# Attention products on 64-column tiles, one logarithm for two head pairs, and other norms

## The chip, the cores and the metric

The kernel runs on one core of one Trainium2 chip. A core has a matrix engine (TensorE, PE in the profile; its weight loads are shown as PEld), three engines for vectors (VectorE, DVE; ScalarE, ACT; GpSimd, POOL), a queue engine (SyncE, SP) and 16 DMA engines. The engines run side by side, each through its own instructions in the order in which they were written, and wait for one another by semaphores. Matmuls read SBUF and write PSUM, which has eight banks of 512 floats per partition. The metric is device time in microseconds (us). The median of three runs of the kernel before is 380.99 us (380.83 to 381.56).

## The reference

Sparse attention, then a feed-forward layer with a periodic activation. Eight batches, eight heads, 576 tokens, 64 columns a head; a token sees its neighbours within 32, and eight global tokens see and are seen by all.

```python
scores = scale * np.matmul(q, k.transpose(0, 1, 3, 2))
mask = np.abs(pos[:, None] - pos[None, :]) <= window
mask = mask | is_global[:, None] | is_global[None, :]
scores = np.where(mask, scores, -1000000000.0)
attn = np.exp(scores - max);  attn = attn / (sum(attn) + 1e-09)
x = np.matmul(attn, v)                  # heads side by side: 4608 x 512
h = x @ w_in                            # 512 x 2048
s = np.sin(alpha * h)
g = h + s * s / (alpha + 1e-09)
out = g @ w_out                         # 2048 x 512
```

## The kernel before, in words

The work goes batch by batch. `attention(b)` makes `xT`, the attention output of batch b with columns on the partitions and the 576 tokens along the free side, in four chunks of 128 columns (two heads, a "head pair", each). `gemm1(b)` multiplies it with `w_in` in 16 groups `nt` of 128 columns, and makes from each the activation in `H2`. `gemm2(b)` multiplies that with `w_out`; it is a generator that gives one matmul of 512 columns at each call, 64 for an even batch and 80 for an odd one. `fill(n)` takes n of them, so the second product of batch b-1 is strewn among the instructions of `attention(b)` and `gemm1(b)`. The counts are written out by hand (`START`, `PER_SCORES`, `LATE`, `MIDST`, `PER_GROUP`, `GROUP_LATE`). What is left over is run after the last batch. There is no planner: the order of the program text is the order on each engine.

Attention takes the keys in 12 blocks of 48, each with the eight global keys and for two heads at once (128 partitions), against 60 query positions of either parity, 120 columns. For head pair `hp` there are three groups `g` of four blocks. `scores(hp, g)` makes four matmuls into one of two `ring` banks (L739), ACT takes the exponential into `E` (L747) and adds it up along the free side into a column of `EA` (its accumulator is read by an instruction of its own), and DVE multiplies with a 0/1 mask (L750).

`products(hp, gs, keys)` (L781) multiplies `E` with the values `VX` (key 0, into PSUM tile `zn`) and with a block matrix of ones `OB` (key 1, the sums, into `zd`), 14 matmuls with 128 columns of weights per pair and key. The last pair uses `zd` and a third tile `zr` in the place of the ring. `inverse(hp)` takes Ln of the sums (L807) and Exp of its negative (L810), again with a row sum into `RA`; `normalise(hp)` (L813) multiplies on DVE into `xT`; `sums` (L791) gathers the parts of the global rows, whose quotient (L862, L863) is `XG`. The pair `hp - 1` is multiplied between the scores of pair `hp`, so one pair is always behind.

In `gemm1`, group `nt` uses `zn`, `zr`, `zd` in turn, the last group `zn`. PE writes a tile in eight matmuls (L969), ACT takes the sine (L1005), ACT or DVE squares it (L1010, L1012), and DVE adds both parts (L1016), which frees the tile. For the last batch 64 columns of global rows (`XG`, L974) ride along.

The sine is exact only for small arguments and the sums must be in range, so the kernel judges itself: `square_x` and `token_norms` (L899 to L910) make the squared norm of each token by squares on DVE and a matmul with ones, `square_w` and `column_norms` (L873, L880) that of each column of `w_in`; `judge` compares these and the row sums, and if they fail, a general path runs instead.

DMA: POOL's queue casts and loads k, q, v, `w_in` (`load_w_in`, L407) and `w_out`; SP's queue transposes k and q, spreads the global values and writes the output (L1042). DVE places the transposed k and q of the next batch (`place`, L347, L354); `beside(at)` puts that and the norms after pair `at`.

## Time and profile before

| | |
|---|---|
| median of three runs | 380.99 us |
| span of the profiled execution | 379.3 us |
| mean granted TensorE clock | 0.994 |
| PE busy | 338.6 us, 89% |
| ACT busy | 294.0 us, 77% |
| DVE busy | 288.8 us, 76% |
| POOL busy | 130.4 us, 34% |

The profiled execution is known by its span, from its first instruction to its last; what lies around it is not in the profile. A row of a group reads: line, engine, operation, output <- inputs, shapes, count | busy us, mean ns of one | idle us before it, and what ended it. A row of the timeline reads: start, duration, engine, line, operation, count, and in brackets the idle time before it with its releaser. Matmuls overlap, and the end of each is modelled, so the distance between starts tells what one costs when many follow each other. A row of busy time by stretch reads: start:end, length, then for PE, PEld, DVE, ACT and POOL busy us and (x instructions), the granted clock, the DMA share, and GB/s.

### The profile page before, as it was taken

The numbers are of one execution on the slowest core, as the hardware profiler recorded it, in microseconds if no ns is written. First come the engines' busy times: TensorE is split into PE (matmuls) and PEld (weight loads), VectorE is DVE, ScalarE is ACT, GpSimd is POOL, SyncE is SP. The second block draws the span as 40 slices with busy tenths as digits, with TensorE's granted clock in tenths as the row PEclk, the third lists the DMA queues.
The fourth block names the chain that finished last, engine by engine and source line by source line (L and its number), as shares of the span: only waits on it lengthen the run. The fifth ranks groups of instructions, "written<-read, shape, count | busy, mean of one in ns | idle before, by whom it ended". The sixth has DMA issues, their size and how long they took to land. (4 is left out here: it accounts for less than half of the span.)

```text
span 379.3 us, 8582 instructions
## 1 busy us (share of the span) xinstructions
PE 338.6 (89%) x3124; PEld 231.9 (61%) x3172; DVE 288.8 (76%) x615; ACT 294.0 (77%) x563; POOL 130.4 (34%) x203
## 2 busy tenths in 40 slices
PE   2578967998998899899989999999999998999893
PEld 2466645765566666676666766676676665775341
DVE  5787897589789887988888788888888876589400
ACT  6889797899889688788878887879788888675110
POOL 7981695677277002840086007720000000000001
PEclk9999999999999999999999999999999999999997
DMA  7998999999988772799069923828111010101221
GB/s 121 117 184 172 152 166 173 170 207 146 204 163 76 134 124 65 92 109 204 28 85 105 193 58 45 84 31 156 50 35 29 0 55 32 29 3 29 56 84 48
DMA packets 103579, 38.08 MB, mean 100 GB/s; under 512 B 94138, under 2 KB 98250, under 8 KB 103082
## 3 DMA queue, kind: packets, MB, share of 16 engines
q0 software_dynamic: 56640, 18.56, 42.2%
q1 hardware_dynamic: 46890, 18.89, 23.1%
q8 instruction: 27, 0.44, 0.5%
q14 instruction: 22, 0.18, 0.2%
HBM read 37.15 MB, written 17.83 MB: 145 GB/s over the span
## 5 line engine op out<-in xcount | busy, mean ns | idle before, releaser
L1029 PE MATMUL zo<-w_out,H 128*128 128x512 bf16 x528 | 142.5, 378 | 2.0
L969 PEld LDWEIGHTS <-w_in 128*128 128x128 bf16 x1024 | 99.2, 97 | 49.3 <-issue 17.6
L390 POOL DMA_DIRECT2D VX<-in_v_dram x128 | 84.0, 667 | 106.5 <-PE zd L781 89.6
L1029 PEld LDWEIGHTS <-H 128*128 128x128 bf16 x576 | 52.0, 97 | 37.3
L747 ACT ACTIVATE E<-ring 128x480 bf16<-128x480 f32 x96 | 54.2, 568 | 23.3 <-PE ring L739 22.8
L969 PE MATMUL zn<-xT,w_in 128*128 128x288 bf16 x384 | 57.3, 285 | 5.6 <-DVE H L1016 4.1
L969 PE MATMUL zr<-xT,w_in 128*128 128x288 bf16 x320 | 47.9, 285 | 1.3 <-DVE H L1016 0.6
L969 PE MATMUL zd<-xT,w_in 128*128 128x288 bf16 x320 | 46.6, 285 | 1.7 <-DVE H L1016 1.7
L750 DVE TENSOR_TENSOR E<-E,MASK 128x480 bf16<-128x480 bf16 x96 | 36.0, 408 | 14.8 <-ACT E L747 13.5
L1016 DVE SCALAR_TENSOR_TENSOR H<-s,recipT,zn 128x576 bf16<-128x576 bf16 x48 | 39.1, 814 | 10.5 <-ACT s L1010 6.2
L1005 ACT ACTIVATE sb<-zn,alphaT 128x576 bf16<-128x576 f32 (+1 forms) x48 | 35.6, 742 | 13.3 <-PE zn L969 9.8
L1057 POOL DMA_INDIRECT out_dram<-osb,grow x1 | 1.0, 1007 | 126.1 <-SPq L1158 126.1
L1010 ACT ACTIVATE s<-sb 128x576 bf16<-128x576 bf16 (+1 forms) x62 | 42.7, 689 | 2.0
L739 PE MATMUL ring<-QX,KX 128*128 128x120 bf16 x384 | 37.2, 221 | 7.1 <-ACT E L747 4.2
L739 PEld LDWEIGHTS <-KX 128*128 128x128 bf16 x384 | 28.2, 100 | 22.0 <-issue 9.0
L1016 DVE SCALAR_TENSOR_TENSOR H<-s,recipT,zd 128x576 bf16<-128x576 bf16 x40 | 32.5, 813 | 6.5 <-ACT s L1010 4.8
L1016 DVE SCALAR_TENSOR_TENSOR H<-s,recipT,zr 128x576 bf16<-128x576 bf16 x40 | 32.5, 813 | 5.0 <-ACT s L1010 2.8
L1012 DVE TENSOR_TENSOR s<-sb 128x576 bf16<-128x576 bf16 (+1 forms) x66 | 30.8, 467 | 7.0 <-ACT sb L1005 6.7
L1035 ACT COPY osb<-zo 128x512 f32<-128x512 f32 x36 | 20.8, 578 | 19.5 <-PE zo L1029 19.4
L1005 ACT ACTIVATE sb<-zd,alphaT 128x576 bf16<-128x576 f32 (+1 forms) x40 | 29.7, 742 | 7.5 <-PE zd L969 4.7
L1005 ACT ACTIVATE sb<-zr,alphaT 128x576 bf16<-128x576 f32 (+1 forms) x40 | 29.6, 740 | 5.1 <-PE zr L969 3.8
L781 PEld LDWEIGHTS <-VX 128*128 128x128 bf16 x448 | 25.9, 98 | 12.2 <-issue 6.7
(157 smaller groups left out, 446.8 us busy)
## 6 DMA issues: line engine op xcount, KB each, us to landing
VX<-in_v_dram POOLq DMA_DIRECT2D x128, 36.0 KB, 3.6
kd<-in_k_dram POOLq DMA_DIRECT2D x7, 576.0 KB, 6.2
qd<-in_q_dram POOLq DMA_DIRECT2D x7, 576.0 KB, 8.9
w_in<-in_moe_w_in_dram POOLq DMA_DIRECT2D x4, 512.0 KB, 5.7
w_out<-in_moe_w_out_dram POOLq DMA_DIRECT2D x4, 512.0 KB, 8.7
out_dram<-osb SPq DMA_DIRECT2D x8, 256.0 KB
out_dram<-osb SPq DMA_DIRECT2D x8, 224.0 KB
out_dram<-osb SPq DMA_DIRECT2D x8, 192.0 KB
```

The lines of the kernel that those rows point to most:

```text
L390: nc.gpsimd.dma_start(out=VX[b % 2][r : r + 24, hp, :, t * D : t * D + D], in_=v[b, 2 * hp + t].rearrange("(i a y) d -> y a i d", a=24, y= ...
L739: nc.tensor.matmul(out=ps[:, e * WCOL : (e + 1) * WCOL], lhsT=kx[:, hp, i, :], rhs=qx[:, hp, :, s0 : s0 + 60], start=True, stop=True, skip ...
L747: nc.scalar.activation(out=Eg, in_=ps[:, 0 : 4 * WCOL], func=AF.Exp, scale=scale, accum_out=EA[:, n : n + 1])
L750: nc.vector.tensor_tensor(out=Eg, in0=Eg, in1=MASK[:, 4 * g : 4 * g + 4, :].rearrange("p i c -> p (i c)"), op=ALU.mult,)
L781: nc.tensor.matmul(out=out_t[:, half, :, a - half * CUT : z - half * CUT], lhsT=OB[:] if key else VXb[:, hp, i, :], rhs=E[:, i, :, a - s0 ...
L969: nc.tensor.matmul(out=h[:, e, 0:HALF], lhsT=lhsT, rhs=xT[:, c, e, :], start=(c == 0), stop=(c == CT - 1), skip_group_check=True,)
L1005: nc.scalar.activation(out=sb[:, :, 0:W], in_=h[:, :, 0:W], func=AF.Sin, scale=alphaT[:, nt : nt + 1])
L1010: nc.scalar.activation(out=s2[:, :, 0:W], in_=sb[:, :, 0:W], func=AF.Square)
L1012: nc.vector.tensor_tensor(out=s2[:, :, 0:W], in0=sb[:, :, 0:W], in1=sb[:, :, 0:W], op=ALU.mult)
L1016: nc.vector.scalar_tensor_tensor(out=dst.rearrange("p (e c) -> p e c", e=2), in0=s2[:, :, lo:hi], scalar=recipT[:, nt : nt + 1], in1=h[:, ...
L1029: nc.tensor.matmul(out=ops[:], lhsT=H2[:, nt, blk * P : (blk + 1) * P], rhs=w_out[:, nt, :], start=(nt == 0), stop=(nt == NT - 1),)
L1035: nc.scalar.copy(out=osb[:], in_=ops[:])
```

## The change

- **Products of two head pairs.** Scores of pairs 0 to 3 are made as before, but products wait until both pairs of a double pair `pp` are there. Key 2 (ones, `OB` now 128 x 64), key 0 (the even columns of the values) and key 1 (the odd ones) each multiply with 64 columns of weights; pair 2pp writes partitions 0 to 63 of a tile, pair 2pp+1 partitions 64 to 127, by turns. One tile of sums thus stands for four heads, and each of two tiles of results holds half of the columns of all four.
- So there are one Ln and one Exp for a double pair, two normalises with the same inverse. Double pair 0 is multiplied after scores 2/1 (keys 2 and 0) and 3/0 (key 1), double pair 1 after 3/1, after 3/2, and after the ring. `E` has four buffers.
- The order of columns in `xT` changes, so `w_in` is loaded by rows in pairs, in 8 transfers where there were 4.
- **Checks.** Exp no longer adds up rows (no `EA`, `RA`). Rows of each logarithm are copied by a DMA on SP's queue into `LC`, which is compared at the end (`judge_sums`), as are the sums of the global rows.
- **Token norms.** `token_norms(b, z)` multiplies `xT` with itself, 20 matmuls into `zn` after pair 0, and takes the largest entry of each row. `square_x` goes. At the end `largest_norm` turns the column of maxima by two small matmuls.
- **w_in squares last.** `square_w` goes from gemm1(1) and attention(2) to the end, between fills; `judge` with its 16 one-column matmuls stands behind all of `gemm2`.
- Global rows: one quotient for all batches, before the last gemm1.
- Fills: `MIDST` 8 for 4 and moved behind the normalises, and 4 (`BEFORE`) between the first chunks of gemm1.

```diff
-    pairp = mctx.enter_context(tc.tile_pool(name="pairp", bufs=2))
+    pairp = mctx.enter_context(tc.tile_pool(name="pairp", bufs=4))
...
     def load_w_in(gs):
         for g in gs:
             cols = slice(g * DFF // 4, (g + 1) * DFF // 4)
-            nc.gpsimd.dma_start(
-                out=w_in[:, :, cols], in_=moe_w_in[:, cols].rearrange("(c p) n -> p c n", p=P)
-            )
+            for q in range(2):
+                nc.gpsimd.dma_start(
+                    out=w_in[:, 2 * q : 2 * q + 2, cols],
+                    in_=moe_w_in[q * DM // 2 : (q + 1) * DM // 2, cols].rearrange("(p k) n -> p k n", k=2),
+                )
...
-            nc.scalar.activation(
-                out=Eg, in_=ps[:, 0 : 4 * WCOL], func=AF.Exp, scale=scale, accum_out=EA[:, n : n + 1]
-            )
+            nc.scalar.activation(out=Eg, in_=ps[:, 0 : 4 * WCOL], func=AF.Exp, scale=scale)
...
-        def nd(hp, key):
-            t = (zn, zd)[key] if hp < NHP - 1 else (pair["zr"] if key else zd)
+        def place_of(pp, key):
+            t = (zd, zn)[pp] if key == 2 else (zn, zd)[pp] if key == 0 else pair["zr"] if pp else zd
...
-                            nc.tensor.matmul(
-                                out=out_t[:, half, :, a - half * CUT : z - half * CUT],
-                                lhsT=OB[:] if key else VXb[:, hp, i, :],
-                                rhs=E[:, i, :, a - s0 : z - s0],
+                        for n in range(2):
+                            hp = 2 * pp + n
+                            bank = (pp, key, half, n)
+                            nc.tensor.matmul(
+                                out=out_t[n * D : (n + 1) * D, half, :, a - half * CUT : z - half * CUT],
+                                lhsT=OB[:] if key == 2 else VXb[:, hp, i, key::2],
+                                rhs=Es[hp][:, i, :].rearrange("p (x c) -> p x c", x=2)[:, :, a - s0 : z - s0],
...
+        def logarithm(pp):
+            Ls[pp] = normp.tile([P, 4, 3, KT], DT.float32, name="L")
+            nc.scalar.activation(out=Ls[pp][:], in_=body(pp, 2), func=AF.Ln)
+            r0 = b * H + 4 * pp
+            nc.sync.dma_start(
+                out=LC[r0 : r0 + 4, :], in_=Ls[pp][0 : P : D // 2].rearrange("p k m c -> p (k m c)")
+            )
...
         for hp in range(NHP):
             Es[hp] = pairp.tile([P, NT12, WCOL], DT.bfloat16, name="E")
...
+            scores(hp, 0)
+            fill(per_scores[hp][0])
+            idle(hp)
+            if hp == 3:
+                products(0, range(3), 1)
+                sums(0, 1)
+                normalise(0, 1)
+            scores(hp, 1)
+            fill(per_scores[hp][1])
+            idle(hp)
+            if hp == 2:
+                products(0, range(3), 2)
+                logarithm(0)
+                sums(0, 2)
+                products(0, range(3), 0)
+            if hp == 3:
+                products(1, range(2), 2)
             scores(hp, 2)
+            if hp == 2:
+                inverse(0)
+                sums(0, 0)
+                normalise(0, 0)
+            if hp == 3:
+                products(1, range(2), 0)
             idle(hp)
...
             fill(per_scores[hp][2])
...
-        products(last, range(3), (1,))
-        inverse(last)
+        products(1, (2,), 2)
+        logarithm(1)
+        inverse(1)
         nc.scalar.preload_act_table(AF.Sin)
-        sums(last, 1)
+        sums(1, 2)
+        products(1, (2,), 0)
+        products(1, range(3), 1)
+        sums(1, 0)
+        normalise(1, 0)
+        sums(1, 1)
+        normalise(1, 1)
+        beside(3)
         fill(MIDST)
-        products(last, range(3), (0,))
-        sums(last, 0)
-        normalise(last)
...
+    def token_norms(b, z):
+        xf = xTs[b][:].rearrange("p c e s -> p c (e s)")
+        for lo, m, n in [(i * P, i * P, P) for i in range(4)] + [(S - P, 4 * P, S - 4 * P)]:
+            for c in range(CT):
+                nc.tensor.matmul(
+                    out=z[:, m // 512, m % 512 : m % 512 + n], lhsT=xf[:, c, lo : lo + P], rhs=xf[:, c, m : m + n],
+                    start=(c == 0), stop=(c == CT - 1), skip_group_check=True,
+                )
+        nc.vector.tensor_reduce(
+            out=XC[:, b : b + 1], in_=z[:].rearrange("p k n -> p (k n)")[:, 0:S], axis=AX.X, op=ALU.max
+        )
...
-                for n in range(2):
-                    chunks(n, range(CT - 1))
+                chunks(0, range(2))
+                fill(BEFORE)
+                chunks(0, range(2, 3))
+                chunks(1, range(3))
...
             if at == 0:
-                if b_moe == 2:
-                    column_norms(zn[:, 0, :])
-                if b_moe >= 3:
-                    token_norms(b_moe - 3, zn[:, 1, :])
-            if 0 <= at < 2 and b_moe:
-                square_x(b_moe, at)
+                token_norms(b_moe, zn)
...
     waiting.append(gemm2(B - 1))
-    square_x(B - 1, 0)
-    square_x(B - 1, 1)
-    fill(32)
-    for n, b in enumerate(sorted(SR)):
-        token_norms(b, (zn, zd)[n % 2][:, 0, :])
-    global_norms(zd[:, 0, :])
+    token_norms(B - 1, zn)
+    global_norms(zd)
+    judge_sums()
     fill(16)
-    judge(zn[:, 0, :])
+    xm = largest_norm(zd)
+    for c in range(CT):
+        square_w(c)
+        fill(16)
+    judge(zn, xm)
     fill(2 * NT * NT)
     gemm2_globals()
```

More of the change, by code (lines that the diff above doesn't have):

```diff
@@ L134, in general_path @@
                 qT, kT = tr
-                xn = wk.tile([KW, NKT, 2, D], DT.bfloat16, name="g_xn")
+                if not second:
+                    xn = wk.tile([KW, NKT, 4, D], DT.bfloat16, name="g_xn")
                 for h in range(2):
@@ L928, in judge @@
[L928 to L939 removed]
+        nc.vector.tensor_tensor(out=c2[:], in0=z[:, 0, 0:NT], in1=c2[:], op=ALU.mult)
@@ L943, in judge @@
-        nc.vector.tensor_copy(out=verdict[:], in_=pv[:, 0:1])
+        nc.vector.tensor_reduce(out=okb[:], in_=oks[:], axis=AX.X, op=ALU.min)
+        nc.tensor.matmul(out=z[:, 1, 0:1], lhsT=ones[:], rhs=okb[:], start=True, stop=True)
+        nc.vector.tensor_copy(out=verdict[:], in_=z[:, 1, 0:1])
     ON_ACT = (1, 3, 5, 8, 10, 12, 14)
@@ L1075 @@
     LATE = ((0, 0, 0), (0, 0, 0), (2, 3, 3), (4, 4, 6))
-    MIDST = 4
+    MIDST = 8
+    BEFORE = 4
     PER_GROUP = (0, 0, 5) + 11 * (1,) + (0, 0)
```

249 lines of the change are left out of this document (109 added, 140 removed).

## The prediction

> **What bounds the kernel now.** I read the page's head first, then busy time by stage, then the list of PE's waits, then single stages in time. Stage names: att(b) is attention of batch b with the second product of b-1 filled in, gemm1(b) the first product; a stage starts with its first score or w_in matmul.
>
> ```profile
> span 379.3 us, 8582 instructions
> PE 338.6 (89%) x3124; PEld 231.9 (61%) x3172; DVE 288.8 (76%) x615; ACT 294.0 (77%) x563; POOL 130.4 (34%) x203
> ```
>
> PE leads, but 89% is a mean over unlike stages. Columns below: start:end, length, then busy us of PE, weight load, DVE, ACT, POOL. In order: att(0), gemm1(0), att(1), gemm1(1), att(2), gemm1(2), att(4), gemm1(4), att(6), tail.
>
> ```profile
> 16.11:33.28 17.17, 13.82 (x166) 11.45 (x166) 14.14 (x37) 15.24 (x43) 10.25 (x13) 1.00 1.20 160
> 33.28:55.70 22.42, 18.15 (x137) 12.86 (x136) 19.57 (x36) 19.48 (x29) 15.92 (x24) 1.00 1.20 172
> 55.70:73.05 17.35, 15.04 (x189) 10.70 (x193) 11.96 (x33) 14.27 (x38) 10.13 (x17) 1.00 1.40 174
> 73.05:99.16 26.11, 24.80 (x170) 16.42 (x171) 22.81 (x37) 24.18 (x34) 19.15 (x31) 1.00 1.41 176
> 99.16:119.72 20.56, 19.03 (x208) 12.52 (x211) 15.99 (x34) 18.30 (x41) 10.98 (x16) 1.00 0.95 157
> 119.72:141.81 22.09, 20.28 (x148) 14.21 (x149) 18.80 (x32) 17.93 (x28) 3.71 (x6) 1.00 0.74 115
> 182.23:202.10 19.87, 18.83 (x211) 12.59 (x213) 16.72 (x37) 16.20 (x41) 10.86 (x16) 1.00 0.51 63
> 202.10:222.42 20.32, 19.85 (x147) 14.21 (x148) 16.84 (x28) 17.02 (x26) 3.60 (x6) 1.00 0.87 143
> 262.71:281.55 18.84, 18.67 (x210) 12.60 (x213) 15.43 (x37) 15.76 (x41) 0.00 (x0) 1.00 0.25 56
> 345.55:372.88 27.33, 25.67 (x120) 11.60 (x121) 9.22 (x33) 4.96 (x10) 0.00 (x0) 1.00 0.24 69
> ```
>
> From about 140 us on, PE fills its stages (18.67 of 18.84, 19.85 of 20.32) at a granted clock of 1.00, with ACT and DVE at 80 to 85%. There a microsecond of PE work is a microsecond of time, and one taken from ACT or DVE is worth only what PE waited for it. Before 140 us PE is free for 3.35, 4.27, 2.31, 1.31, 1.53 and 1.81 us of the six stages: 14.6 us. The list of waits has one that recurs in the later attention stages (total, times, longest):
>
> ```profile
> PE zn L781 <- DVE xT L813: 3.4, 5, 0.9
> ```
>
> **Part 1, products.** Before: per batch 4 pairs x 2 keys = 8 units of 14 matmuls with 128 columns of weights. After: 2 double pairs x 3 keys (sum, even columns, odd columns) = 6 units of 14 twins, each twin two matmuls with 64 columns of weights, one to either half of the partitions.
>
> ```profile
> 199.98 0.79 PE L781 MATMUL zr<-E,OB 128*128 128x88 bf16 x14
> 200.61 1.03 PE L1029 MATMUL zo<-w_out,H 128*128 128x512 bf16 x4
> ...
> 340.22 0.18 PE L974 MATMUL zn<-XG,w_in 128*128 128x32 bf16 x1
> 340.25 0.28 PE L969 MATMUL zn<-xT,w_in 128*128 128x288 bf16 x1
> ...
> L1051 PEld LDWEIGHTS <-HG x16: 106/110/110, 369.2 to 372.2; 128*64 128x64 bf16 x16
> ...
> L781 PEld LDWEIGHTS <-OB x448: 95/97/147, 19.0 to 319.1; 128*128 128x128 bf16 x150
> ```
>
> A unit of today takes 200.61 - 199.98 = 0.63 us, so 8 x 0.63 = 5.04. No row shows a twin. Lower bound: a twin costs what one matmul does, 0.63 for a unit. Upper bound: the two run one after the other, 1.26. A row between: a matmul of 32 columns with its own load starts 0.03 us before the next (340.22 to 340.25); if that is the least a load with its matmul takes, 28 of them take 0.84, and nearer 0.7 if part of that step is streaming. And loads do not shrink: the 64-column one is recorded with 110 ns, the 128-column one with 97. I take 0.74, nearest to these two rows: 6 x 0.74 = 4.44, a gain of 0.60 per batch.
>
> The Trainium skill, "TensorEngine Tiling (Array Packing)", Feature Incompatibilities, says that column tiling excludes the fast weight load, which speaks against this change; the 110 against 97 ns above agrees. No run here shows two of them following each other on short matmuls.
>
> **Changing the tile form.** Only the last product today uses 64 columns of weights.
>
> ```profile
> 199.12 0.38 PE L1029 MATMUL zo<-w_out,H 128*128 128x512 bf16 x1
> ...
> 367.77 1.46 PE L1029 MATMUL zo<-w_out,H 128*128 128x512 bf16 x6
> ...
> 369.16 0.79 PEld L1051 LDWEIGHTS <-HG 128*64 128x64 bf16 x5 [0.42 <-issue]
> 369.16 1.05 PE L1051 MATMUL zo<-w_out,HG 128*64 128x512 bf16 x4
> ```
>
> One matmul of 512 columns is recorded with 0.38 us and six with 1.46, so they start (1.46 - 0.38) / 5 = 0.216 apart, and the seventh's turn is at 369.07; the first 128*64 load comes only at 369.16 (0.42 us of idle loader, while elsewhere loads run ahead). So 0.09 us per change of form. The new order has five blocks of twins per batch (after scores 2/1; after 3/0; after 3/1; after 3/2; after the ring is released), ten changes: bounds 0 (each beside a wait) to 10 x 0.12, I take 0.9.
>
> **Part 2, token norms.** One L908 matmul of 288 columns (0.12) goes; 16 matmuls of 128 columns and 4 of 64 come.
>
> ```profile
> 198.30 0.37 PE L739 MATMUL ring<-QX,KX 128*128 128x120 bf16 x4
> 198.51 0.36 PE L781 MATMUL zn<-E,VX 128*128 128x120 bf16 x4
> ...
> L899 DVE TENSOR_TENSOR SQ<-xT 128x2304 bf16<-128x2304 bf16 x8 | 10.8, 1351 | 0.0
> ...
> L813 DVE TENSOR_TENSOR xT<-zn,R 128x576 bf16<-128x576 f32 x24 | 18.1, 754 | 7.5 <-ACT R L810 7.3
> ...
> L750 DVE TENSOR_TENSOR E<-E,MASK 128x480 bf16<-128x480 bf16 x96 | 36.0, 408 | 14.8 <-ACT E L747 13.5
> ...
> L747 ACT ACTIVATE E<-ring 128x480 bf16<-128x480 f32 x96 | 54.2, 568 | 23.3 <-PE ring L739 22.8
> ...
> L747 ACT ACTIVATION_READ_ACCUMULATOR E<-ring 128x1 f32 x96 | 19.0, 198 | 0.0
> ...
> L807 ACT ACTIVATE L<-zd,tiny 128x576 f32<-128x576 f32 x24 | 17.7, 736 | 0.0
> ...
> L810 ACT ACTIVATE R<-L 128x576 f32<-128x576 f32 x32 | 21.9, 683 | 1.0
> ...
> L873 ACT ACTIVATE SQ<-w_in 128x2048 bf16<-128x2048 bf16 x3 | 5.7, 1903 | 0.0
> ...
> L407 POOL DMA_DIRECT2D w_in<-in_moe_w_in_dram x4: 762/790/872, 12.0 to 37.4; - x4
> ```
>
> Four matmuls of 120 columns take 0.21, so 128 columns about 0.056 and 64 about 0.04: 16 x 0.056 + 4 x 0.04 = 1.06, net +0.94 on PE per batch. DVE loses the squares (1.35 us and their three adds) and gains one reduction of 576 (0.75, by the L813 row).
>
> **Part 3, fewer logarithms.** ACT loses all 96 accumulator reads, two of four Ln (0.74) and two of four Exp (0.68) per batch, by busy time 12 x 0.2 + 2 x (0.74 + 0.68) = 5.2 us of some 40. In att(3) to att(7) I count that at nothing: PE, at 18.67 of 18.84, hides it; were PE not the bound, it would be worth up to those 5.2. What does change is the wait for xT (longest 0.9, in att(3) to att(5)): it goes, but the double pair 2/3 needs the mask product of scores 3/1, which stands on DVE behind the sums and the normalise of the double pair 0/1 (0.75, then 0.41 for itself), and these wait for products that PE finished only one block of scores (0.21) and four fills (0.86) before. That is late next, by 0.3 to 0.8 us. I take zero for both together.
>
> So att(3) to att(7): -0.60 + 0.9 + 0.94 = +1.24 each, **+6.2**. gemm1(3) to (6) lose RG and XG, which DVE does ahead of their first H; PE is free for 0.47 us in such a stage (20.32 - 19.85), and I give 0.2 of it back: **-0.8**, bounds 0 and -1.9. The BEFORE and MIDST fills only move matmuls (18 fewer are left for the end) and are worth nothing by themselves.
>
> **The early stages.** att(2) with gemm1(2): +1.24, but squares of w_in and xT leave ACT and DVE; gemm1(2) is 1.8 us longer than gemm1(4), and I give that back and 0.5 more: **-1.1**. att(1) with gemm1(1): the norms' reduction stands ahead of the place copies, the fills are moved to the border, two ACT squares go: **-0.4**. att(0) has no fills, so its length is a chain: scores 3/2 now stand behind the sums of the double pair 2/3, and then come Exp 0.57, mask 0.41, the last third of a unit, Ln 0.74, Exp 0.68 and two normalises of 0.75 where one was: 1.3 us longer; **+1.3**. The 5.2 us that ACT loses in it are the other bound. w_in comes in 8 transfers, not 4, on POOL's queue, ahead of the VX loads and of kd and qd; products are later than the VX landings, so 0 (with that cover gone 4 issues at up to 0.79, 3 us). The 16 small transfers of logarithms on SP's queue wait for an Ln and hold back the output behind them; osb has three buffers, so 0.
>
> **The tail.**
>
> ```profile
> 345.55 6.85 PE L1029 MATMUL zo<-w_out,H 128*128 128x512 bf16 x31
> ...
> 348.11 0.27 DVE L1016 SCALAR_TENSOR_TENSOR HG<-s,recipT,zn 128x64 bf16<-128x64 bf16 x1
> ...
> 352.24 0.29 PE L908 MATMUL zn<-SR,ones 128*128 128x288 bf16 x1
> ...
> 354.79 3.62 PE L1029 MATMUL zo<-w_out,H 128*128 128x512 bf16 x15
> ...
> L675 DVE TENSOR_SCALAR far<-qpos,fone 128x576 bf16<-128x576 f32 x1 | 0.8, 777 | 0.1
> ...
> L937 DVE TENSOR_REDUCE ok<-cmp 128x1 f32<-128x96 f32 x1 | 0.3, 254 | 0.0
> ```
>
> Today 32 matmuls run while DVE drains, then norms take PE from 352.24 to 354.79: 2.5. After, token_norms(7) is PE's first work and writes zn, which DVE reads until 348.38: a wait of 2.8, then 1.0 of matmuls. Beside 16 fills (3.45) DVE has the reduction 0.75, judge_sums (four passes of 576 at about 0.75 and four short ones at 0.25: 4.0) and two small ones, so the transpose in largest_norm waits 1.6 and its row 0.6. The squares of w_in lie beside 64 fills and cost nothing; without that cover, four of 1.9 us. Behind all fills judge has 16 one-column matmuls (0.5) and a DVE chain of 1.2 that PE waits out before the global product: 2.8 + 1.0 + 1.6 + 0.6 + 0.5 + 1.2 - 2.5 = **+5.2**, bounds +2 and +7.
>
> **Sum.** 6.2 - 0.8 - 1.1 - 0.4 + 1.3 + 5.2 = +10.4 on a span of 379.3: 389.7. The profile holds the span only; the median of the runs, 380.99, is 1.7 above it, so 391.4.
>
> **Rivals.** *Twins run wholly together* (0.63 a unit): 6 x 0.11 in six attentions, -4.0: 387.4, and down to 382.0 if the ten changes also hide. For it: the loads overlap in every row above. Against: the 0.03 us step.
> The Trainium skill, "TensorE: Matmul & The Clock Gate", Part 3, gives a pack the time of one matmul and about 4 ns per further tile; by that a unit would be an estimated 0.69 and the sum about 389.6. No run of before shows it.
> *Twins run one after the other* (1.26): 6 x 0.52 x 6 = +18.7: 410.1. For it: nothing in the trace shows two at a time. Against: nothing shows that they can't.
> *The other side: the waits for ACT and DVE go.* The free PE time of the six early stages, 14.6, and 1.0 in each of att(3) to att(5) by the row of att(4), is 17.6. My sum takes back 3.5 of it and is +13.9 without. If the relief of ACT and DVE takes back more than 13.9, the kernel is faster; with all of it, 391.4 - 14.1 = 377.3. For it: gemm1(0), att(0) and gemm1(1) have ACT at 87 to 93%. Against: gemm1(0) loses no ACT or DVE work.
>
> **How the numbers follow.** Forecast 0.42 (its own range 386 to 397, from the tail's bounds and 0.7 to 0.84 a unit), wholly together 0.17, one after the other 0.16, the other side 0.22, no change 0.03. A measurement here tells about 0.2% from none, 0.8 us. Slower 0.75, the same 0.03, faster 0.22. The range leaves out half of the serial case and a quarter of the other side: 376 to 405.
>
> **What would show it.** A unit of twins in time (0.63, 0.74 or 1.26); a gap where 128*128 turns to 128*64; att(4) 1.2 us longer beside its added fills; 2.8 us before the first norm matmul of the tail and 1.2 before the global product. Wrong if att(0) to gemm1(2) come out more than 5 us shorter.

## The result and the profile after

The changed kernel takes 408.28 us (median of four runs, 406.01 to 409.41), the kernel before on the same chip 381.27 (median of four). The ratio is 1.068, with a 95% interval of 1.061 to 1.074: slower, as forecast, but by 27 us where the forecast had 10, and outside its range. A profiled execution of the changed kernel has a span of 405.4 us, 26.1 more than before, and its own time is 407.24. Ratios, and the times of the experiments below, leave out executions that took over 1.5% longer than the fastest of the same kernel: one of the kernel before here (386.74 us), and one or two of each of six kernels below, up to 421 us.

The head of the page after:

```profile
span 405.4 us, 9591 instructions
PE 350.3 (86%) x3729; PEld 231.8 (57%) x3774; DVE 266.0 (66%) x547; ACT 264.4 (65%) x403; POOL 130.5 (32%) x207
```

ACT lost 29.6 us of busy time and DVE 22.8, as meant. PE has 11.7 us more work, but the span grew by 26.1, so more than half of the loss is PE standing still. Busy time by stage, after; the columns are those of the forecast's table, the stages att(0), gemm1(0), att(1), gemm1(1), att(2), gemm1(2), att(4), gemm1(4), att(6):

```profile
16.09:34.72 18.63, 13.30 (x223) 10.00 (x222) 13.03 (x35) 12.14 (x25) 11.74 (x15) 0.93 1.28 171
34.72:58.89 24.17, 18.30 (x139) 13.05 (x138) 21.23 (x35) 19.52 (x28) 18.34 (x28) 0.98 1.18 161
58.89:79.73 20.84, 18.07 (x269) 11.89 (x274) 12.30 (x33) 11.39 (x19) 13.29 (x22) 0.92 1.44 174
79.73:105.58 25.85, 23.61 (x163) 15.96 (x165) 18.77 (x30) 20.14 (x31) 14.45 (x23) 1.00 1.18 170
105.58:127.86 22.28, 20.69 (x288) 12.94 (x293) 12.01 (x29) 12.74 (x21) 7.95 (x13) 1.00 0.62 103
127.86:149.86 22.00, 20.87 (x150) 14.58 (x151) 18.03 (x29) 16.79 (x26) 5.92 (x10) 1.00 0.95 143
194.19:215.99 21.80, 20.69 (x288) 12.93 (x293) 12.48 (x31) 12.74 (x21) 7.47 (x12) 1.00 0.29 47
215.99:237.99 22.00, 20.87 (x150) 14.57 (x151) 16.86 (x27) 16.79 (x26) 6.68 (x11) 1.00 1.06 144
282.31:304.13 21.82, 20.70 (x288) 12.93 (x293) 12.48 (x31) 12.74 (x21) 0.00 (x0) 1.00 0.14 38
```

PE no longer fills the later stages. In att(6) it was free for 0.17 us before and is for 1.12 now; in gemm1(4) for 0.47 before and for 1.13 now, and that stage has 22.0 us in every batch from 2 to 6. The stages against the forecast (us; all eight batches, the stage starts read from the timeline):

| stage | forecast | measured |
|---|---|---|
| att(0) | +1.3 | +1.5 |
| gemm1(0) | 0 | +1.8 |
| att(1) with gemm1(1) | -0.4 | +3.2 |
| att(2) with gemm1(2) | -1.1 | +1.6 |
| att(3) to att(7) | +6.2 | +11.4 |
| gemm1(3) to gemm1(6) | -0.8 | +6.9 |
| gemm1(7), tail | +5.2 | +0.9 |
| before the first and behind the last matmul | 0 | -1.1 |
| sum | +10.4 | +26.1 |

The tail's 0.9 is not like for like: by the counts in the program, the fills that the change puts into earlier stages leave 24 matmuls of 0.216 us less for gemm1(7) and what follows it (90 in place of 114), some 5 us. With the numbers of fills of before (the second experiment) this stage is 5.8 longer than in the kernel before, where 5.2 were forecast. The difference lies in the stages above it.

What PE waits for now (list of waits after: total, times, longest); in the list of before neither of the first two kinds comes to more than 0.8 us:

```profile
PE ring L738 <- DVE H L1045: 8.0, 7, 1.7
...
PE zn L776 <- DVE E L746: 6.6, 8, 1.2
...
PE zn L905 <- DVE HG L1045: 2.9, 1, 2.9
...
PE zn L973 <- DVE okb L972: 1.0, 1, 1.0
```

And where they stand (timeline of PE after):

```profile
237.97 0.80 PE L738 MATMUL ring<-QX,KX 128*128 128x120 bf16 x8 [0.95 <-DVE H L1045]
...
247.44 0.83 PE L776 MATMUL zd<-E,OB 128*64 128x88 bf16 x28
248.11 1.02 PE L776 MATMUL zn<-E,VX 128*64 128x88 bf16 x28
...
251.10 0.83 PE L776 MATMUL zd<-E,VX 128*64 128x88 bf16 x28
251.86 0.38 PE L738 MATMUL ring<-QX,KX 128*128 128x120 bf16 x4
...
253.04 0.71 PE L776 MATMUL zn<-E,OB 128*64 128x88 bf16 x9
254.94 0.41 PE L776 MATMUL zn<-E,OB 128*64 128x120 bf16 x11 [1.18 <-DVE E L746]
...
282.30 0.37 PE L738 MATMUL ring<-QX,KX 128*128 128x120 bf16 x4 [1.08 <-DVE H L1045]
...
329.99 1.17 PE L905 MATMUL zn<-xT 128*128 128x128 bf16 x20
331.00 0.37 PE L738 MATMUL ring<-QX,KX 128*128 128x120 bf16 x4
```

Four things are to be seen. A unit of 28 half-width matmuls takes 248.11 - 247.44 = 0.67 us where another unit of twins follows, hardly more than the 0.63 of 14 full ones before: the twins run together. Where matmuls of full width follow, it takes 251.86 - 251.10 = 0.76, with the change of form at its end. The 20 norm matmuls take 331.00 - 329.99 = 1.01. The first scores of an attention wait about 1 us for DVE's last-but-one `H`. And the products of the second double pair wait 1.2 us for a mask product.

The first of the two waits comes from an edit that neither my list of the change nor my prediction has: in `gemm1` the three PSUM tiles are taken in the order `zn`, `zd`, `zr`, not `zn`, `zr`, `zd`. So group 14, the last but one, stands in the tile `zr`, whose banks the ring of the next attention takes; before, it was group 13.

Why every gemm1 has 22.0 us shows in two of them, gemm1(5) and gemm1(4) (busy time by stretch, after):

```profile
260.29:282.31 22.02, 19.64 (x141) 13.56 (x141) 16.97 (x27) 17.26 (x27) 7.54 (x12) 1.00 0.69 100
215.99:237.99 22.00, 20.87 (x150) 14.57 (x151) 16.86 (x27) 16.79 (x26) 6.68 (x11) 1.00 1.06 144
```

In gemm1(5) the fills run out and PE has 1.2 us less to do, and the stage is no shorter. By this, gemm1 is a chain of groups here (matmuls, sine, square, `H`, then the tile is free), and a fill inside it is free as long as the chain is the longer. A fill moved out of that chain into an attention, or ahead of gemm1's first group, costs its 0.216 us in full, as the second experiment shows.

### The profile page after: what moved, and what is told of

Read it like the earlier page. It is cut to its first block, busy times and chain, and to the rows that moved or that the text cites. A ratio compares the mean times of both kernels' runs of the same rounds, so it can differ in the third digit from the quotient of the medians.

```text
span 405.4 us, 9591 instructions
## 1 busy us (share of the span) xinstructions
PE 350.3 (86%) x3729; PEld 231.8 (57%) x3774; DVE 266.0 (66%) x547; ACT 264.4 (65%) x403; POOL 130.5 (32%) x207
## 4 chain that ended last, share of the span: by engine, by line
PE 56%; DVE 14%; ACT 10%; DMA 7%; issue 6%; POOL 4%; SPq 0%; POOLq 0%; DVEq 0%; ACTq 0%
PE zo L1058 25%; PE zd L1000 6%; PE zn L1000 6%; DVE H L1045 6%; PE zr L1000 5%; PE ring L738 5%; ACT sb L1034 5%; PE zd L776 4%; DMA w_in<-in_moe_w_in_dram 3%; PE zn L776 3%; ACT s L1039 2%; PE zn L905 2%; DMA kd<-in_k_dram 2%; DVE xT L816 2%; POOL VX L389 2%
## 5 line engine op out<-in xcount | busy, mean ns | idle before, releaser
L1058 PE MATMUL zo<-w_out,H 128*128 128x512 bf16 x531 | 139.9, 380 | 2.7 <-issue 1.4
L746 DVE TENSOR_TENSOR E<-E,MASK 128x480 bf16<-128x480 bf16 x96 | 40.0, 425 | 39.4 <-ACT E L745 38.4
L1000 PE MATMUL zn<-xT,w_in 128*128 128x288 bf16 x384 | 58.8, 286 | 3.5 <-DVE H L1045 2.7
L1000 PE MATMUL zd<-xT,w_in 128*128 128x288 bf16 x320 | 47.9, 285 | 3.6 <-DVE H L1045 2.8
L1000 PE MATMUL zr<-xT,w_in 128*128 128x288 bf16 x320 | 46.6, 285 | 2.2 <-DVE H L1045 1.1
L738 PEld LDWEIGHTS <-KX 128*128 128x128 bf16 x384 | 26.6, 100 | 31.6 <-issue 16.2
L1064 ACT COPY osb<-zo 128x512 f32<-128x512 f32 x36 | 20.9, 581 | 17.0 <-PE zo L1058 17.0
L776 PEld LDWEIGHTS <-VX 128*64 128x64 bf16 x896 | 24.5, 115 | 4.6 <-issue 3.2
```

The lines of the kernel that those rows point to most:

```text
L738: nc.tensor.matmul(out=ps[:, e * WCOL : (e + 1) * WCOL], lhsT=kx[:, hp, i, :], rhs=qx[:, hp, :, s0 : s0 + 60], start=True, stop=True, skip ...
L746: nc.vector.tensor_tensor(out=Eg, in0=Eg, in1=MASK[:, 4 * g : 4 * g + 4, :].rearrange("p i c -> p (i c)"), op=ALU.mult,)
L776: nc.tensor.matmul(out=out_t[n * D : (n + 1) * D, half, :, a - half * CUT : z - half * CUT], lhsT=OB[:] if key == 2 else VXb[:, hp, i, key ...
L1000: nc.tensor.matmul(out=h[:, e, 0:HALF], lhsT=lhsT, rhs=xT[:, c, e, :], start=(c == 0), stop=(c == CT - 1), skip_group_check=True,)
L1058: nc.tensor.matmul(out=ops[:], lhsT=H2[:, nt, blk * P : (blk + 1) * P], rhs=w_out[:, nt, :], start=(nt == 0), stop=(nt == NT - 1),)
L1064: nc.scalar.copy(out=osb[:], in_=ops[:])
```

## The experiments

Two theories stand against one another. *Order theory*: what is lost beyond the forecast is an order of tiles, fills and DVE work in which PE waits. *Work theory*: it is PE's added work.

**The order of tiles in gemm1**

```diff
-                hs[nt] = (zn, zd, None)[nt % 3] or hr.tile([P, 2, 512], DT.float32, name="zr")
+                hs[nt] = (zn, None, zd)[nt % 3] or hr.tile([P, 2, 512], DT.float32, name="zr")
```

> The changed kernel with one edit: gemm1 takes its PSUM tiles in the old order zn, zr, zd, not zn, zd, zr, so that the last group but one does not stand in the banks that the first scores of the next attention use. Order theory (the loss beyond my forecast is an order of tiles and fills that makes PE wait): the 1.0 us wait of the first scores for H at each of seven attention starts goes, 5 to 8 us less than the changed kernel's 408.3. It may cost up to 0.3 us each, since group 1 then waits for the last normalise. Work theory (the loss is PE's added work: norm matmuls, changes of form): within 1 us of 408.3.

Measured: 397.4 to 403.0 us, ratio to the kernel before 1.045 (1.038 to 1.053); 5 to 11 us less than the changed kernel. The wait of the ring is gone from all but two places, and gemm1(4) falls from 22.00 to 20.89 with the same PE work (list of waits, then busy time of att(4) and gemm1(4), of this kernel):

```profile
PE ring L738 <- DVE H L1045: 1.7, 2, 1.2
```

```profile
201.74:223.60 21.86, 20.70 (x287) 12.95 (x292) 13.45 (x32) 13.81 (x23) 7.46 (x12) 1.00 0.28 47
223.60:244.49 20.89, 20.71 (x149) 14.59 (x150) 15.90 (x25) 15.69 (x24) 6.72 (x11) 1.00 1.09 151
```

The attentions stay as long as they were. So 1.1 us in each of gemm1(2) to gemm1(6), 5.5 together, is that one line's. (The profiled execution, of 412.5 us, has 35.7 us in att(2), where a transpose takes 19.98 us; that comes up again with the four edits. The rows above are clear of it.)

**The numbers of fills of before**

```diff
-    MIDST = 8
-    BEFORE = 4
+    MIDST = 4
+    BEFORE = 0
```

> The changed kernel with the old fills: 4 matmuls of gemm2 after the attention for 8, and none between the first chunks of gemm1 for 4; what is left over runs at the end. Order theory: gemm1 lasts about 19.2 us from its first sine to its end whether 20 or 11 fills lie in it, so fills taken out of it cost their full time elsewhere. Then 8 fewer per batch save 1.7 us in seven batches, and some 20 more at the end cost 4.3: 5 to 8 us less than 408.3, at most the whole lost again if the first chunks wait for the normalises. Work theory, and my forecast (fills only move matmuls): within 1 us of 408.3.

(The middle ones still stand behind the normalises.) Measured: 401.8 and 402.7 us, some 6 us less (too few for a ratio). Busy time of att(4) and gemm1(4) of this kernel:

```profile
189.23:210.26 21.03, 19.82 (x283) 12.58 (x289) 11.63 (x29) 11.72 (x21) 6.65 (x11) 1.00 0.27 47
210.26:231.52 21.26, 20.20 (x146) 14.18 (x147) 17.73 (x29) 17.66 (x26) 7.57 (x12) 1.00 1.17 106
```

The attentions 2 to 6 fall to 20.9 to 21.4 (0.8 to 0.9 each, four fills), gemm1(3) to gemm1(6) to 21.2 to 21.5, and gemm1(7) with the tail grows from 52.6 to 57.5. So matmuls that were moved from a place where they cost nothing to one where they cost all did cost: from att(1) on the stages gain 10.0 us, twice what the tail pays.

**The mask product ahead of the normalise**

```diff
             if hp == 3:
                 products(0, range(3), 1)
+            scores(hp, 1)
+            if hp == 3:
                 sums(0, 1)
                 normalise(0, 1)
-            scores(hp, 1)
```

> The changed kernel with sums and normalise of key 1 of the first double pair moved behind the scores 3/1, so that DVE multiplies the mask of scores 3/1 first. Order theory: PE's wait of 1.2 us inside the products of the second double pair goes in att(2) to att(6) and becomes smaller in att(7): 4 to 7 us less than 408.3. Work theory: within 1 us.

Measured: 404.15 us (404.07 to 405.05), ratio 1.059 (1.054 to 1.064), 4.1 us less. The attentions 3 to 6 are 21.4 long in place of 21.8 to 22.3, att(2) to att(7) together 3.1 us shorter, and the list of waits has

```profile
PE zn L776 <- DVE E L746: 1.3, 2, 0.9
```

in place of 6.6 us in eight. The wait was real, but these stages gained 3.1 us of the 4.7 that it lost in them.

**The order of the tail**

```diff
+    judge_sums()
+    fill(16)
     token_norms(B - 1, zn)
     global_norms(zd)
-    judge_sums()
...
-        fill(16)
+        fill(16 if c < 3 else 0)
```

> The changed kernel with 16 fills put ahead of the last token norms (taken from the last block of fills), and judge_sums ahead of them. Both theories: the 2.9 us wait for HG of the last norm matmuls goes and part of the wait before the transpose: 2 to 4 us less than 408.3, as my forecast had its tail at +5.2.

Measured: 401.5 to 404.9 us, ratio 1.058 (1.050 to 1.065). The stage of gemm1(7) and the tail falls by 3.3 us, from 52.56 to 49.30; the rest of the 3 to 7 us lies ahead of batch 2, in stages that this edit does not touch and that differ by 1 to 2 us between profiles. Of the 5.8 us of the tail, 3.3 were an order in which PE's first work waits for the last `HG`.

**The norms left out**

```diff
             if at == 0:
-                token_norms(b_moe, zn)
+                pass
```

> The changed kernel with the token norms left out of attentions 1 to 7 (the twenty Gram matmuls in zn and their largest value; the last batch and the global rows keep theirs, so seven batches' tokens are not judged). It measures by itself what the norms cost on PE. Work theory: 20 matmuls of 1.01 us a batch and 0.1 to 0.2 us of changes of form, 1.1 to 1.2 us in each of att(1) to att(7) and nowhere else, 7.5 to 8.5 us in all, 398 to 401 against the changed kernel's 408.3. If the norms lie in time that PE would lose anyway (the products behind them wait for DVE's mask product, 1.2 us), the time stays within 2 us of 408.3 and the wait for the mask product grows by as much as the matmuls gave back. Order theory has no stake here except that the first products wait the longer.

Measured: 401.07 us (399.76 to 401.92), ratio 1.052 (1.048 to 1.056): 7.2 us less, 1.0 for each of seven attentions (att(4) 20.83 in place of 21.80). The norms' matmuls lie on the path and cost what they take.

**The twins not in turns**

```diff
-            for g in gs:
+            for g, n in [(g, n) for g in gs for n in range(2)]:
                 for i in range(4 * g, 4 * g + 4):
...
-                        for n in range(2):
-                            hp = 2 * pp + n
+                        hp = 2 * pp + n
```

> The changed kernel with the same product matmuls, but not in turns: of each group of four key tiles first all of the even pair (n = 0, columns 0 to 63 of the array), then all of the odd pair (n = 1, columns 64 to 127). Nothing else is moved. If two twins run beside one another because they stand one behind the other in the stream, this takes it away: a unit of 28 goes from 0.62 to 0.65 us up to about 1.25 us (28 of 44 ns), 24 units a batch of 0.6 us minus what lies under waits, so 6 x 0.62 = 3.7 us a batch and up to 28 us in all, 428 to 437. If PE pays by the columns streamed and not by the neighbour (a half-width matmul costs half whoever stands beside it), the time stays within 2 us of 408.3. Something between says that the queue ahead of the array reaches over a few matmuls only.

Measured: 409.73 us (409.27 to 411.02), 1.5 us more than the changed kernel; an attention is 0.3 us longer. A unit, in the timeline of this kernel:

```profile
206.42 0.95 PE L775 MATMUL zd<-E,VX 128*64 128x88 bf16 x28
207.30 0.38 PE L738 MATMUL ring<-QX,KX 128*128 128x120 bf16 x4
```

28 take 0.88 us with the change of form at the end, against 0.76 for the like unit in the changed kernel and some 1.3 if each ran alone. That the time hardly moves could also mean that a half-width matmul costs half whoever stands beside it. The records of this unit speak against that: the two first matmuls, one of either pair and each the only one of 88 columns among its four, start at 206.416 and 206.429, though three of the even pair stand between them in the text, and in the groups of four those of one half follow one another at 50 to 65 ns. So half-width matmuls on different halves of the array overlap though four to six of one half stand together; the order of the twins costs little, and it is not what the kernel loses by.

**The kernel before without its accumulations**

```diff
+    nc.vector.memset(EA[:], 1.0)
+    nc.vector.memset(RA[:], 1.0)
...
-                out=Eg, in_=ps[:, 0 : 4 * WCOL], func=AF.Exp, scale=scale, accum_out=EA[:, n : n + 1]
+                out=Eg, in_=ps[:, 0 : 4 * WCOL], func=AF.Exp, scale=scale
...
-            nc.scalar.activation(out=Rs[hp][:], in_=L[:], func=AF.Exp, scale=-1.0, accum_out=RA[:, n : n + 1])
+            nc.scalar.activation(out=Rs[hp][:], in_=L[:], func=AF.Exp, scale=-1.0)
```

> The kernel before with its accumulations left out (the exponentials of the scores and of the inverse lose their running sums; what the self-check reads of them is set to 1, so that part of the self-check is empty). ACT loses 128 reads of the accumulator, 25 us of busy time, and nothing else changes. It asks what ACT's relief, which the change brings, is worth by itself. The prediction's rival (ACT and DVE are what PE waits for): 5 to 10 us faster than before, 371 to 376. Work theory and order theory: PE waits for ACT at a few places only (gemm1's chain has no accumulation in it, and the ring has three banks), 0 to 3 us, 378 to 381.

Measured: 379.31 us against 381.38, ratio 0.9945 (0.9918 to 0.9972). (The ring has two banks, not three.) Busy time by engine, of this kernel:

```profile
PE 341.2 (90%) x3172; PEld 232.9 (62%) x3172; DVE 290.0 (77%) x617; ACT 283.2 (75%) x435; POOL 129.6 (34%) x203
```

A third of the change's relief of ACT, 10.8 us by busy time (294.0 to 283.2), is worth 2.1 us in the kernel before. (The accumulator's own rows add up to 25 us; only 10.8 of them leave the busy time, so they overlap with their neighbours.) The relief counts for something, though not in batches 0 and 1, where the rival looked for it (39.7 and 44.0 us, before 39.6 and 43.5); it is far from the 14 that my rival on the other side asked for, but the other two thirds, and DVE's relief, are not in this run.

**The four edits of order together**

The diffs of the first four experiments in one kernel.

> The changed kernel with all four edits of order together: gemm1's tiles back to zn, zr, zd; four fills in the middle and none ahead of gemm1; scores (3, 1) ahead of the last products of the first two pairs; judging of the sums and 16 fills ahead of the last token norms. Order theory: the four gains were 8, 6, 4 and 4 us one by one; ring and fills act on the same group chain in gemm1 and the late sums on the same wait as the fills do not, so 15 to 22 us of the 27 come back: 386 to 393, still above the kernel before by PE's work (norm matmuls 8, changes of form 8, less 7.5 for the products). Work theory (the edits of order only share one gain): 397 to 402.

Measured: 407.4 to 412.2 us, ratio 1.075 (1.066 to 1.084). No gain at all, where both theories expected one. The trace shows why: from att(2) to gemm1(6) the other nine stages are as short as the order theory has them (20.5 to 21.2; att(4) 20.53, gemm1(4) 20.70), and att(5) has 36.14 us. The timelines of SP, DVE and PE there:

```profile
212.71 16.23 SPq L336 DMA_TRANSPOSE kt<-kd  x1
229.04 18.86 SPq L336 DMA_TRANSPOSE qt<-qd  x1
...
247.94 0.92 DVE L353 COPY KX<-kt 64x1152 bf16<-64x1152 bf16 x2 [18.56 <-DMA kt<-kd]
...
240.57 0.37 PE L906 MATMUL zn<-xT 128*128 128x64 bf16 x4 [8.36 <-issue]
...
249.36 0.20 PE L776 MATMUL zd<-E,OB 128*64 128x88 bf16 x1 [2.19 <-DVE E L746]
```

The transposes of k and q for the next batch take 35 us where 5 are usual; DVE, at the place copies of `kt`, waits 18.6 us for them, and its mask products stand behind. PE itself stands at "issue" for 8.4 us among the norm matmuls. There the DMA rows show a packet of the queue of instructions at 238.2 to 239.1, the first of that queue since 203.9, and PE goes on at 240.6; so PE probably waited for its own instructions, whose transfer was late too. No run tests it. With att(5) at its neighbours' length the time would be 392. POOL issued the casts of the batch after next 0.4 us behind the first transpose. Over the profiles of all kernels up to here and of the next three, past the first 90 us, the time of `kt` goes with the distance of the two issues: 15 to 20 us where the transpose was issued 0.1 to 0.4 us ahead of the casts, 8 to 11 where the casts were 0.3 to 1.7 us ahead, 5 to 9 at 2.4 to 4.3, and 2.2 to 3.5 with no cast near, or with the casts 1 to 2.7 us behind (in att(1), where they also fall together, it takes 4 to 6). The changed kernel itself has 11.31 us at a distance of 0.63, and its place copies do not wait for it; the earlier kernel has 7.38 at 2.61.

**One buffer for the casts**

```diff
+    dram1 = mctx.enter_context(tc.tile_pool(name="dram1", bufs=1, space=bass.MemoryType.DRAM))
...
-            t = dramp.tile([P, H * S * D // P], DT.bfloat16, name=name)
+            t = (dramp if b < 3 else dram1).tile([P, H * S * D // P], DT.bfloat16, name=name)
```

on top of the four edits; the same without the norms; and on the changed kernel alone.

> The kernel with all four edits of order, and for batches 3 and later the bf16 copies of q and k in DRAM have one buffer each in place of two. So the casts of batch b + 1 wait for the transposes of batch b to have read theirs, and no longer run beside them. In the kernel with four edits the transposes of one batch took 16.23 and 18.86 us and one attention 36.1 us where its neighbours take 20.5. Theory of the transfers (the transposes are late because the casts and the copies of v crowd the DMA engines at the same time): transposes of 2 to 6 us, every attention 20.2 to 20.9 us, 390 to 393 us, all runs within 1.5%. If the copies of v alone crowd them, or if transposes are late for another reason: still 404 to 418, with an attention of over 25 us in most runs. Order theory: 386 to 393 as said for the four edits; work theory 397 to 402.

> As the kernel above (four edits of order, casts behind the transposes), with the token norms left out of attentions 1 to 7 too (seven batches' tokens are not judged). What is left above the kernel before is then the tail, the changes of form and the places that no edit undid. From the kernel above it takes 7 us (the norms alone gave 408.3 - 401.1 = 7.2 in the changed kernel): 383 to 386, still 2 to 5 us above the 381.4 of the kernel before, if the order theory has the whole cause. At 388 or more the norms hide behind waits again; at 380 or less the products on 64 columns are a gain by themselves that the rest of the change had eaten.

> The changed kernel with the casts behind the transposes and nothing else. Its profiled execution shows transposes of 6.6 to 11.3 us in three batches, but no wait of DVE for them in the list of waits. Theory of the transfers as a cause of the fast runs' loss: 400 to 405. Theory that the transfers only make the disturbed runs: 406 to 409 with the transposes at 2 to 6 us, and the runs closer to one another (406.0 to 409.4 so far).

Measured: 410.9 to 414.3, 405.7 to 410.2 and 405.7 to 408.6 us. The edit did not do what it says: the casts are issued in the same places as before, 0.4 us behind the transpose in the first two kernels and 0.6 ahead in the third. So these three say nothing on the question. They repeat it: in the first two, att(5) has 45.5 and 38.3 us with `kt` at 17.28 and 16.05 us, and the third is the changed kernel once more (406.85).

**The transposes ahead of gemm1**

The four edits, and the transposes where they fall clear of the casts:

```diff
             load_v(b + 2, range(1, NHP))
+            if b > 2:
+                turn_qk(b + 2)
             load_vg(b + 2)
...
-            elif b + 2 < B:
+            elif b < 3:
                 turn_qk(b + 2)
```

and the casts of batch 4 behind the first copies of its v.

> The kernel with all four edits of order, and SP's transposes of batches 5 to 7 ahead of gemm1 in place of behind it (they stand on SP ahead of the copies of the global v rows and wait for nothing but the last place copies); the casts of batch 4 go behind the first four copies of v. The one-buffer edit of the runs before did not hold the casts back: they are issued at the same places in the rows. In all profiles so far the transpose of kt took 14.8 to 20.0 us in the five cases past 90 us in which SP issued it 0.1 to 0.4 us ahead of POOL's casts, 8 to 11.3 us where the casts were 0.3 to 1.7 us ahead, 5.4 to 8.7 us where they were 2.4 to 4.3 us ahead, and 2.2 to 3.5 us where none was within 8 us. Theory of the collision: with the transposes some 6 us ahead of the casts they take 2 to 5 us each, no attention takes over 21 us but the first two, 390 to 394. If the transposes are late for another reason (the copies of v, the state of the chip): an attention of 30 us or more again, 404 to 418.

Measured: 394.77 us (394.25 to 395.50), ratio 1.033 (1.028 to 1.038). The timelines of SP and POOL at the place of the collision:

```profile
207.09 2.91 SPq L336 DMA_TRANSPOSE kt<-kd  x1
210.10 3.91 SPq L336 DMA_TRANSPOSE qt<-qd  x1
...
215.01 0.53 POOL L327 DMA_DIRECT2D kd<-in_k_dram  x1
```

The casts now come 7.9 us behind the transposes, which take 2.9 and 3.9 us, and att(5) has 20.69. Ten copies of v are issued from 206.4 to 212.7, beside the transposes, so it is not these that slow them. The distance of transposes and casts was the cause. All four edits of order give 13.5 us together, less than they gave one by one (5 to 11, 6, 4.1 and 3 to 7): the tiles and the fills shorten the same chain (gemm1(4) 22.00 us in the changed kernel, 20.89 with the one, 21.26 with the other, 20.70 with both).

**And without the norms**

> As the kernel above with the token norms left out of attentions 1 to 7 (seven batches' tokens are not judged). The stages of the earlier kernel without norms, its one long attention put at its neighbours' length, add up to 385. Order theory with the norms as the rest: 382 to 386, 0 to 4 us above the kernel before. At 380 or less the products on 64 columns are a net gain once the order and the norms are undone; at 388 or more something else of the change costs PE time that no run has named.

Measured: 387.88 us (387.22 to 389.89), ratio 1.017 (1.012 to 1.022). That is 6.9 less, the norms' price again, and 2 to 6 more than expected. 6.1 us stay above the kernel before. Batches 2 to 6 are not among them: att with gemm1 of these five add up to 202.8 us here and 202.7 in the kernel before. Batches 0 and 1 are 2.5 longer, and gemm1(7) with att(7) and the tail 4.0. So what is left of the change, the products on 64 columns with their changes of form above all, brings nothing in the batches where PE is the bound, and what it does to the first batches and to the tail is a loss. That it is the products alone is not shown: att(3) to att(5), where the wait for `xT` is gone, are 0.3 to 0.6 shorter than before, att(6), which had no wait to lose, is 0.7 longer, and gemm1(3) to gemm1(6) are 0.4 to 0.8 longer. Part of the last is the price of the old order of tiles, for group 1 now waits for the last normalise (list of waits, of this kernel; before there is 0.3 us of this kind):

```profile
PE zr L1001 <- DVE xT L816: 2.8, 7, 0.4
```

## Why the prediction was wrong

The direction and the bound held: PE is what the later stages go by, and work on PE costs its time. The size fell. Of the 27 us, 13.5 were order (the four edits with the transposes clear of the casts) and 6.9 norms, which the forecast had at nearly that; 6.1 are left. So what failed is the terms of order, which the prediction had at zero or below: the fills, gemm1's tiles and the mask product.

**The fills.** "The BEFORE and MIDST fills only move matmuls ... and are worth nothing by themselves": wrong, by some 5 to 6 us. I had quoted that gemm1 has PE busy for 19.85 of 20.32 and took it for PE's own length. In the changed kernel the stage is as long with 19.64 us of PE work as with 20.87: it has the length of a chain that passes through ACT and DVE, with fills in its gaps. Each fill moved out of there left a hole that nothing filled and took its own time elsewhere.

**gemm1's tiles.** "gemm1(3) to (6) lose RG and XG ...: -0.8": measured +6.9. The step had no place for the order of tiles, which the diff holds and which I passed over. Putting it back gave 5 to 11 us, 1.1 of the 1.7 by which each of these stages had grown. Beside the norms it is the largest single piece, and it could have been read: the last but one `H` now stands in the tile that the ring takes.

**The mask product.** The step named the new wait rightly ("late next, by 0.3 to 0.8 us") and then took "zero for both together". The wait is 1.2 us long, the wait that it replaces was 0.9 at most in three attentions, and undoing it shortened att(2) to att(7) by 3.1 us together. DVE after, from the place copies to the mask product that PE waits for:

```profile
251.45 0.46 DVE L353 COPY KX<-kt 64x1152 bf16<-64x1152 bf16 x1
251.94 0.92 DVE L346 COPY QX<-qt 64x1152 bf16<-64x1152 bf16 x2
252.89 0.41 DVE L746 TENSOR_TENSOR E<-E,MASK 128x480 bf16<-128x480 bf16 x1
253.21 0.22 DVE L787 TENSOR_REDUCE GN<-zd 128x8 f32<-128x64 f32 x1
253.35 0.75 DVE L816 TENSOR_TENSOR xT<-zd,R 128x576 bf16<-128x576 f32 x1
254.01 0.87 DVE L746 TENSOR_TENSOR E<-E,MASK 128x480 bf16<-128x480 bf16 x1
```

I had counted the sums, the normalise and 0.41 for the mask product. I had not counted the three place copies, 1.4 us, which stand ahead of these and of the mask product before and make DVE late for all of them, and the mask product itself is recorded with 0.87 us here.

**The early stages.** att(0) was right (+1.3, measured +1.5). The rest (-1.5 for gemm1(0) to gemm1(2)) came out at +6.6. I gave back time there because ACT and DVE lost work. The accumulations' 10.8 us of ACT work, taken out of the kernel before, return 2.1, so that part of the relief is worth a fifth of its busy time. With order and norms undone, batches 0 to 2 are 1.0 longer than before in place of 8.1, so most of the loss here is the same as in the later batches; what stays lies in batches 0 and 1 (2.5 longer, batch 2 is 1.5 shorter), and which step makes it stays open.

**The products.** 0.74 us a unit was too dear: by the distances of starts in the timeline, PE's time for products fell from 4.84 to 3.9 us a batch, 0.94 and not 0.60, if the waits inside the units are left out (in att(5) 0.2 and 0.3 us beside the one of 1.2). The rival with the twins wholly together was right on this term. The Trainium skill, "TensorE: Matmul & The Clock Gate", Part 3, whose rule I had worked out to an estimated 0.69, was nearer than my term, and the trace has still less. The warning that I took from the Trainium skill, "TensorEngine Tiling (Array Packing)", Feature Incompatibilities, did not show: the loads of 64 columns are recorded at 115 ns, and they are not what a unit takes.

**The changes of form** cost about 1.1 us an attention by the starts in the timeline (forecast 0.9), and **the norms** 1.01 (forecast 0.94 net). Both held. Together they eat the products' gain twice over.

**The tail** nearly held: +5.8 on like work where 5.2 were forecast, with the 2.9 us wait for `HG` (forecast 2.8) and 1.0 for `judge`'s chain (1.2). The wait ahead of the transpose was 0.6 (forecast 1.6) and that for its row 0.3 (0.6). With these sizes the forecast's sum would be 3.8; the other 2 us of the 5.8 stay open.

**The rivals.** The one with the serial twins gives 410.1, next to the result, by a mechanism that is false: that a number fits says nothing for its story. The one on the other side looked for its gain in the first batches, and these are 2.5 us longer than before even with order and norms undone and with all of the relief of ACT and DVE. The case that came true, new waits in several places, each of which I had either priced at zero or not seen, was none of mine.

What stays open: what in the DMA engines makes a transpose so slow beside the casts, and why it matters which was issued first. And whether the 8.4 us in which PE stands at "issue" in the collision are a wait for instructions, as the DMA rows suggest.

## What to carry to other kernels

A stage in which the bound engine is 98% busy can still be a chain through other engines with filler in its gaps: before pricing a moved filler at zero, take a stage where the filler runs out and see whether it gets shorter. Read every hunk of a diff for what it does to the order in which buffers come free; the one line on the tile order cost nearly as much as all the matmuls of the norms. And when several repairs that work singly give nothing together, look for one stage that has become much longer before giving up the theory: here a transfer slipped into the time of another.

## What the runs showed of the hardware

- Two half-width matmuls on different column halves start 3 to 9 ns apart in the records and cost little more than one matmul's time (28 in 0.67 us, 14 full ones in 0.63), down to 32 streamed columns, each with a fresh load; with four to six of one half together, 28 take only 0.12 us more.
- A DMA transpose of 576 KB, that of k, takes 2.2 to 4.5 us where no cast is issued within 8 us of it and 15 to 20 (the one behind it up to 26) when the casts of another batch are issued 0.1 to 0.4 us behind it; the first cast then lands after 15 to 40 us in place of 5 to 9. The Trainium skill, "DMA: Bandwidth & Descriptors", Queues, rings and completion order, says that an engine takes packets from its queues by turns. The milder cases agree with a mere sharing: 2.9 us and some 6 make the 8 to 11 that were measured with the cast ahead. The 15 to 20 with the transpose ahead are more than the sum, and sharing by turns does not explain them.
- In such a stall the granted clock falls (0.75 in the 5 us from 235 and 0.57 in the 5 us from 240 in the kernel with four edits), and four matmuls of 120 columns are recorded with 0.59 us where 0.37 is usual.
